# A gated linear attention kernel with two matmuls behind it: k turned by VectorE and put in order by way of DRAM, masks moved to ScalarE and GpSimd, a rounding moved behind the first scores

## The chip, the cores and the metric

The kernel runs on one core of a Trainium2 chip. The metric is the time of one execution in microseconds (us), the median of some runs. In profiles, PE is TensorE's matmuls, PEld its weight loads, DVE VectorE, ACT ScalarE, POOL GpSimd, SPq and ACTq the DMA issues in the streams of SyncE and ScalarE. L483 is a line of the kernel. The change shifts lines: the scores are L757 before and L770 after, the values L800 and L821, the states L815 and L837.

## The reference, cut to what matters

```python
def _attn_ref(q, k, v, alpha):          # (4, 8, 768, 48): batch, heads, tokens, head size
    state = np.zeros((B, H, D, D)); y = np.zeros_like(q)
    for t in range(S):
        state = alpha[:, :, t, :, None] * state + np.einsum('bhd,bhe->bhde', k[:, :, t], v[:, :, t])
        y[:, :, t] = np.einsum('bhd,bhde->bhe', q[:, :, t], state)
    return y
# x = y with the heads side by side: (3072, 384)
def _moe_ref(x, w_in, w_out):           # (384, 2048), (2048, 384)
    h = x @ w_in
    return ((h / (1 + np.exp(-h))) @ w_out)
```

## The kernel before

The tokens are cut into 24 chunks of 128 (6 per sequence, 4 sequences). For each chunk VectorE builds kp (k divided by its decay) and qp (q times its decay). Then TensorE does **scores** (kp times qp, masked to the causal half), **values** (masked scores times v, plus the running state times qp) and **states** (kp times v, added to the running state). The states need kp with tokens on partitions, so it has to be turned. Between these short pieces, one piece of the two big matmuls after another is put in, called `enter` (x times w_in) and `leave` (times w_out) here. From chunk 8 on (`NA`) the chunks run in a steady pattern.

```python
def scores(n):
    ps = c.pop("blank") if n >= NA else [ps_attn() for _ in range(2)]   # ps_attn: a ring of 3 PSUM buffers
    ...                                                                  # cut: 16 matmuls into ps
    for u in range(2):
        ...                                                              # cut: first chunks
        dve.tensor_tensor(g[:, u], ps[u], mask, ALU.mult)                # views cut
    if ci < NCH - 1:
        ps_k = ps_attn()
        for j in range(NP):
            pe.transpose(ps_k[:, j, :], c["kp"][:, j, :], ident)         # k turned by TensorE
        c["kn"] = work.tile([128, NP, C], F32, name="kn")
        act.copy(c["kn"], ps_k)

def load_v(n):                       # the v of chunk n, one of two buffers, three DMAs
    t = c["v"] = vns[n % NV]         # NV = 2: waits until the states of chunk n - 2 have read it
    nc.sync.dma_start(t[:, 0 : H // 2, 0:D], x[:, 0 : H // 2])
    ...

for step in range(STEPS):            # from chunk 8 on, in the order of the program:
    stages = [[(scores, 1)], [(products, 0)], [(values, 1), (states, 1)], [(quotient, 0), (blank, 0)]]
    for slot, group in enumerate(stages):
        for stage, lag in group:
            n = step - lag
            stage(n)
            if stage is quotient and n + 1 < NT: load(n + 1)      # alpha, k, q: 12 DMAs
            if stage is states and n + NV < NT: load_v(n + NV)
        fill(step, slot)             # pieces of the big matmuls
```

Two things here matter later. All these loads, and the stores of the output, are issued by **SyncE**, one after another. And the order of the program is not the order of an engine's instructions: when the kernel is built, each engine gets its own fixed order (the built order), which can change when the program does. How the builder chooses it was not looked into. On the chip, each engine goes through that order and waits where it must.

Of the kernel before, what the change touches and what calls it, by code (L numbers as in the profile page):

```python
# [8 lines left out]
F32 = mybir.dt.float32  # L9
# [346 lines left out]
def quotients(  # L356
# [22 lines left out]
    C = 128  # L379
# [27 lines left out]
    opool = pool("opool", 2)  # L407
    rpool = pool("rpool")
    upool = pool("upool")

# [118 lines left out]

    mask = consts.tile([128, 2, C], F32, name="mask")  # L530
    gps.memset(mask, 1.0)
    for odd in range(2):
        for e in range(2):
            m = mask[CH * e : CH * e + CH, odd, :]
            gps.affine_select(m, m, pattern=[[1, C]], compare_op=ALU.is_ge, fill=0.0,
                              base=-CH * (e ^ odd), channel_multiplier=-1)

# [56 lines left out]
    def weights(which):  # L594
# [18 lines left out]
        for i, (dst, src) in enumerate(pieces):  # L613
            if not wide:
                act.dma_start(dst, src)
                yield
                continue
            assert which == 0 or conv_done[0] == n_conv[0]
            bits = coming.pop(0)
            up = ahead.pop() if ahead else rounding(bits)  # L620
            hi, w = bits[:, :, 1], dst.bitcast(I32)
            tc.keep_in_program_order(
                dve.tensor_scalar(w, hi, 3, 0x3FFFFFFF, ALU.logical_shift_left, ALU.bitwise_and))
            dve.scalar_tensor_tensor(w, hi, -(1 << 30), w, ALU.bitwise_and, ALU.bitwise_or)
            dve.tensor_tensor(w, w, up, ALU.add)  # L625
            if i + 1 < len(pieces):
                ahead.append(rounding(coming[0]))
            fetch()
            yield
# [104 lines left out]

    def blank(n):

        if n < NA:
            return
        ps = ctxs[n]["blank"] = [ps_attn() for _ in range(2)]
        for t in ps:  # L740
            act.activation(t.rearrange("p j c -> p (j c)"), ident[:, 0:1].to_broadcast([128, 4 * C]),
                           AF.Copy, scale=0.0)

    def scores(n):
        c = ctxs[n]
        ci, b = c["ci"], c["b"]
        ps = c.pop("blank") if n >= NA else [ps_attn() for _ in range(2)]



        for j in (0, 2, 1, 3):
            for e in range(2 if n >= NA else 1):
                for u in range(2):
# [4 lines left out]
                              start=True, stop=True)  # L758
        g = c["g"] = work.tile([128, 2, NP, C], F32, name="g")
        for u in range(2):  # L760
            if n < GB:

                act.copy(g[:, u], ps[u])
                gps.affine_select(g[:, u], g[:, u], pattern=[[0, NP], [1, C]], compare_op=ALU.is_ge,  # L764
                                  fill=0.0, base=0, channel_multiplier=-1)
                continue
            m = mask[:, :, None, :] if n >= NA else mask[:, 0:1, None, :]
            dve.tensor_tensor(g[:, u].rearrange("p (o j) c -> p o j c", o=2),  # L768
                              ps[u].rearrange("p (o j) c -> p o j c", o=2),
                              m.to_broadcast([128, 2, NP // 2, C]), ALU.mult)  # L770
        if ci < NCH - 1:
            ps_k = ps_attn()
# [12 lines left out]
    def values(n):  # L785

        c = ctxs[n]
        ci, b, g, qp = c["ci"], c["b"], c["g"], c["qp"]
        vn = c["v"].rearrange("p (j u) d -> p j (u d)", u=2)
        s = st[b].rearrange("p j u e -> p j (u e)")  # L790
        py = ps_attn()
        todo = [(3 * j + i, vn[:, j, at : at + 32], g[:, u, j, :])
                for j in range(NP) for i, at, u in ((0, 0, 0), (1, 32, 0), (2, 80, 1))]
        todo += [(3 * j + 1, vn[:, j, 48:80], g[:, 1, j, :]) for j in range(NP)]
        if ci > 0:
# [10 lines left out]
    def states(n):  # L806
        c = ctxs.pop(n)
        ci, b, vn = c["ci"], c["b"], c["v"]
        if ci < NCH - 1:

            ps = ps_attn()
            for j in range(NP):
                for i in range(4):
                    r = slice(32 * i, 32 * i + 32)
                    pe.matmul(ps[r, j, 0:D], lhsT=c["kn"][:, j, r], rhs=vn[:, 2 * j + i // 2, 0:D],  # L815
                              start=True, stop=True)
# [288 lines left out]
    def settle():  # L1105

        first.close()
        late.update(look=pool("look"), part=pool("part"), xc=pool("xc"), turn=pool("turn"),
                    wx=pool("wx").tile([128, 8, NQ, 128], F32, name="wx"))
        quads = pool("quads")  # L1110
# [5 lines left out]
    def fill(step, slot):  # L1116

        at = step * SLOTS + slot
        if at < marks[0]:
            if step >= 1:  # L1120
                convert(0, (at - SLOTS) * 3 // (marks[0] - SLOTS) + 1)
            return
# [10 lines left out]
    for step in range(STEPS):  # L1133
# [6 lines left out]
        elif step >= NA:  # L1140
            stages = [[(scores, 1)], [(products, 0)], [(values, 1), (states, 1)], [(quotient, 0), (blank, 0)]]
        for slot, group in enumerate(stages):
            for stage, lag in group:
# [10 lines left out]
                if stage is states and n + NV < NT:  # L1154
                    load_v(n + NV)
            fill(step, slot)
            if step * SLOTS + slot >= NA * SLOTS - 1 and conv_done[1] == NFT and not late:
# [21 lines left out]
    ps = ps_attn()[0:1, 0, 0:1]  # L1179
    pe.matmul(ps, lhsT=good, rhs=mask[:, 0, C - 1 : C], start=True, stop=True)  # L1180
    dve.tensor_single_scalar(small, ps, 127.5, ALU.is_ge)
# [62 lines left out]
```

## Time and profile before

| what | before |
|---|---|
| time, median of 3 runs | 564.57 us |
| span of the profiled run | 561.6 us |
| TensorE busy | 543.9 us, so 17.7 us without a matmul |
| TensorE busy, 125 to 185 / 185 to 365 / 365 to 445 us | 60.00 / 179.26 / 80.00 us |
| VectorE, ScalarE, GpSimd busy | 453.0, 205.3, 15.1 us |

The prediction below shows the page's main lines. Two views that it didn't show also belong here. The first is the timeline of TensorE in the kernel before; the columns are start, length, engine, line, output and inputs, and count.

```profile
243.29 0.90 PE L757 MATMUL ps_a<-p,kp 48*64 48x128 f32 x32
244.12 0.66 PE L774 MATMUL ps_a<-ident,kp 128*128 128x128 f32 x4
...
255.09 1.08 PE L800 MATMUL ps_a<-g,vn 128*32 128x128 f32 x32
255.99 0.84 PE L800 MATMUL ps_a<-p,st 128*32 128x128 f32 x24
256.65 0.52 PE L815 MATMUL ps_a<-vn,kn 128*32 128x48 f32 x32
```

Scores and k's transposes come first, then 10.5 us of big matmuls (244.6 to 255.1), then the values, and the states directly behind them. The masking has those 10.5 us. The second is what SyncE's queue waits for (line waited for: us in total, times, longest):

```profile
SPq L996 <- DVE o L994: 72.2, 32, 5.9
...
SPq L482 <- PE ps_a L815: 31.0, 13, 5.1
```

L482 is the load of v; in 13 steps it stands at the head of SyncE's queue until the states (L815) have released its buffer, 5.1 us at most. L996 stores the output, which waits for VectorE.

### The profile page before, as it was taken

Reading aid. Unit: us, or ns where it says so; the run is one execution under the profiler, and the core shown is the slowest. Engines: PE = TensorE matmul, PEld = TensorE weight load, DVE = VectorE, ACT = ScalarE, POOL = GpSimd, SP = SyncE. Lnnn points to the kernel's source line nnn. Section 1 sums busy time; section 2 is a strip of 40 time slices with the busy share of each in tenths; the row PEclk is TensorE's granted clock in tenths of the full one; section 3 lists DMA queues with packets and bytes.
Section 4 is the critical chain, followed back from the end, with each engine's and each line's share of the span. In section 5 each row is a group of like instructions: output and inputs, shape, how many; then the busy total and the mean of one; then the engine's idle time right before and its main releaser. Section 6 shows DMA issues by size and latency. Waiting matters only on the chain.

```text
span 561.6 us, 12420 instructions
## 1 busy us (share of the span) xinstructions
PE 543.9 (97%) x5074; PEld 492.6 (88%) x5074; DVE 453.0 (81%) x829; ACT 205.3 (37%) x406; POOL 15.1 (3%) x36
## 2 busy tenths in 40 slices
PE   5899999999999999999999999999999999999996
PEld 3688887998999999899989999999998999899995
DVE  5797899966999799986998897899895875857731
ACT  2566543213233342443433443434443342332100
POOL 4211000100000000000000000000000000000000
PEclk9899999999999999999999999999999999999998
DMA  9989971143443333333425544435522123334200
GB/s 206 230 241 223 234 183 34 43 126 100 100 107 89 73 97 87 101 87 85 131 70 160 142 108 134 130 81 153 136 69 81 53 85 118 99 94 125 71 30 26
DMA packets 94417, 63.81 MB, mean 114 GB/s; under 512 B 55312, under 2 KB 86032, under 8 KB 94352
## 3 DMA queue, kind: packets, MB, share of 16 engines
q1 hardware_dynamic: 94352, 62.94, 43.3%
q8 instruction: 41, 0.67, 0.5%
q14 instruction: 24, 0.20, 0.1%
HBM read 58.20 MB, written 4.72 MB: 112 GB/s over the span
## 4 chain that ended last, share of the span: by engine, by line
PE 75%; DVE 14%; DMA 5%; SPq 2%; issue 2%; ACT 1%; POOL 0%; DVEq 0%; ACTq 0%
PE ps_o L980 33%; PE ps_m L882 18%; PE ps_m L858 11%; PE ps_a L800 6%; DMA bits<-in_moe_w_out_dram 3%; PE ps_a L757 3%; DVE seen L663 2%; PE ps_a L774 1%; DVE g L896 1%; DMA bits<-in_moe_w_in_dram 1%; DVE u L699 1%; PE ps_a L815 1%; DVE w_out L625 1%; DVE p L728 1%; SPq L456 1%
## 5 line engine op out<-in xcount | busy, mean ns | idle before, releaser
L980 PE MATMUL ps_o<-w_out,g 128*128 128x192 f32 x768 | 133.6, 328 | 1.1 <-DVE o L994 1.1
L980 PEld LDWEIGHTS ps_o<-w_out,g 128*128 128x128 f32 x768 | 125.5, 190 | 3.9 <-DVE o L994 1.5
L980 PE MATMUL ps_o<-wt,g 128*128 128x192 f32 x576 | 100.0, 327 | 0.0
L980 PEld LDWEIGHTS ps_o<-wt,g 128*128 128x128 f32 x576 | 95.1, 190 | 1.5
L858 PE MATMUL ps_m<-xt,w_in 128*128 128x256 f32 x384 | 88.5, 382 | 1.0 <-ACT xt L805 1.0
L858 PEld LDWEIGHTS ps_m<-xt,w_in 128*128 128x128 f32 x384 | 71.0, 190 | 11.0 <-ACT xt L805 1.4
L882 PE MATMUL ps_m<-xc,w_in 128*128 128x256 f32 x288 | 70.1, 379 | 0.0
L882 PEld LDWEIGHTS ps_m<-xc,w_in 128*128 128x128 f32 x288 | 54.0, 190 | 6.4 <-DVE g L896 0.2
L663 DVE TENSOR_REDUCE seen<-bits 128x1 f32<-128x384 int32 (+2 forms) x65 | 42.4, 689 | 16.8 <-DMA bits<-in_moe_w_out_dram 16.5
L893 ACT ACTIVATE g<-g 128x1024 f32<-128x1024 f32 x32 | 33.1, 1055 | 57.5 <-DVE g L896 57.5
L985 DVE TENSOR_TENSOR g<-g 128x512 f32<-128x512 f32 x72 | 48.5, 686 | 5.6 <-PE ps_o L980 5.6
L882 PE MATMUL ps_m<-xc,wx 128*128 128x256 f32 x192 | 50.1, 383 | 0.0
L888 ACT COPY g<-ps_m 128x512 f32<-128x512 f32 x64 | 36.8, 587 | 36.1 <-PE ps_m L882 36.0
L780 ACT ACTIVATE st<-st,least 128x96 f32<-128x96 f32 x80 | 24.1, 364 | 58.4 <-DVE least L702 58.4
L882 PEld LDWEIGHTS ps_m<-xc,wx 128*128 128x128 f32 x192 | 35.0, 190 | 4.2 <-issue 0.4
L896 DVE TENSOR_TENSOR g<-ps_m,g 128x512 f32<-128x512 f32 x56 | 37.4, 683 | 0.8 <-PE ps_m L882 0.5
L699 DVE TENSOR_TENSOR_SCAN u<-al,one 128x516 f32<-128x516 f32 x24 | 29.1, 1212 | 10.4 <-ACT al L696 10.3
L728 DVE TENSOR_TENSOR_SCAN p<-al,inv 128x516 f32<-128x516 f32 x24 | 29.4, 1226 | 5.2 <-PE ps_a L800 4.9
L861 ACT ACTIVATE g<-ps_m 128x512 f32<-128x512 f32 x32 | 19.0, 595 | 39.2 <-PE ps_m L858 39.0
L800 PE MATMUL ps_a<-g,vn 128*32 128x128 f32 x768 | 28.0, 282 | 3.9 <-POOL g L764 3.9
L800 PEld LDWEIGHTS ps_a<-g,vn 128*32 128x32 f32 x768 | 20.3, 112 | 11.2 <-issue 5.5
L768 DVE TENSOR_TENSOR g<-ps_a,mask 128x512 f32<-128x512 f32 x40 | 25.7, 685 | 4.0 <-PE ps_a L757 3.7
(125 smaller groups left out, 620.7 us busy)
## 6 DMA issues: line engine op xcount, KB each, us to landing
bits<-in_moe_w_in_dram SPq DMA_DIRECT2D x24, 512.0 KB, 4.7
bits<-in_moe_w_out_dram SPq DMA_DIRECT2D x32, 384.0 KB, 3.4
at<-in_alpha_dram SPq DMA_DIRECT2D x64, 96.0 KB, 2.4
kt<-in_k_dram SPq DMA_DIRECT2D x64, 96.0 KB, 2.6
qt<-in_q_dram SPq DMA_DIRECT2D x64, 96.0 KB, 2.5
bits<-in_alpha_dram SPq DMA_DIRECT2D x9, 512.0 KB, 3.8
out_dram<-o SPq DMA_DIRECT2D x48, 96.0 KB, 1.9
an<-in_alpha_dram SPq DMA_DIRECT2D x8, 192.0 KB, 5.1
```

Of the source, the lines that this page charges most:

```text
L663: dve.tensor_reduce(seen[kind][which][:, i : i + 1], x, axis=AX, op=op, apply_absolute_value=True))
L699: dve.tensor_tensor_scan(u[:, end - 1 :: -1], sg[:, end:0:-1], one[:, end:0:-1], 0.0, ALU.mult, ALU.add)
L728: dve.tensor_tensor_scan(p[:, 0:end], sg[:, 0:end], iv[:, 0:end], 0.0, ALU.mult, ALU.add)
L768: dve.tensor_tensor(g[:, u].rearrange("p (o j) c -> p o j c", o=2), ps[u].rearrange("p (o j) c -> p o j c", o=2), m.to_broadcast([128, 2, ...
L800: pe.matmul(py[32 * at : 32 * at + 32, t, :], lhsT=w, rhs=x, start=(i < 4), stop=(i >= len(todo) - 4), skip_group_check=True)
L858: pe.matmul(ps[:, e, :], lhsT=w_in[:, t, (f + e) * 128 : (f + e + 1) * 128], rhs=xt[:, t, :], start=(t == 0), stop=(t == NKT - 1))
L882: pe.matmul(ps[:, e], lhsT=block_w(w)[:, 2 * pair + e], rhs=block_x(grp, x), start=(first and e == 0), stop=(e == 1), skip_group_check=True)
L888: act.copy(to, ps)
L893: act.activation(x, x, AF.Silu)
L896: dve.tensor_tensor(to, a, b, op)
L980: pe.matmul(ps, lhsT=x, rhs=w[:, i], start=(first and i == 0), stop=(i == HF - 1), skip_group_check=True)
L985: dve.tensor_tensor(cells(grp, h, pair, *to), cells(grp, h, pair, *x), cells(grp, h, pair, *y), ALU.subtract)
```

## The change

Its intent is to take work off TensorE and VectorE. (1) From chunk 8 on, k is turned by VectorE in 32x32 blocks (`flip`) instead of by TensorE; a store to DRAM and four loads (`land`) put the blocks in order. (2) The causal mask is made by ScalarE's copies and GpSimd's selects instead of VectorE's multiplications. (3) At the start, one rounding of weights is traced behind the first scores.

```diff
+    dram = pool("dram", 2, bass.MemoryType.DRAM)
@@ the weights' conversion
             up = ahead.pop() if ahead else rounding(bits)
+            if which == i == 0:
+                yield
@@
-    def blank(n):                              # cut: its body
+    def flip(n):
+        c = ctxs[n]
+        if n < NA or c["ci"] == NCH - 1:
+            return
+        t = late["flip"].tile([128, 4, NP, 32], F32, name="flip")
+        dve.transpose(t, c["kp"].rearrange("p j (c i) -> p c j i", i=32))
+        c["flip"] = dram.tile([128, NP * C], F32, name="flips")
+        nc.sync.dma_start(c["flip"], t.rearrange("p c j d -> p (c j d)"))
+    def land(n):
+        c = ctxs[n]
+        if "flip" in c:
+            c["kn"] = work.tile([128, NP, C], F32, name="kn")
+            x = c.pop("flip").rearrange("(r d) (i x) -> i d r x", r=4, i=4)
+            for i in range(4):
+                nc.sync.dma_start(c["kn"][32 * i : 32 * i + 32], x[i])
@@ scores
-            m = mask[:, :, None, :] if n >= NA else mask[:, 0:1, None, :]
-            dve.tensor_tensor(...)             # cut: g = ps * m
-        if ci < NCH - 1:
+            x = ps[u].rearrange("p (o j) c -> p o j c", o=2)
+            act.copy(swapped[:, :, u, :, CH:], x[:, :, :, CH:])
+            for r, o in earlier:
+                act.copy(swapped[r, o, u, :, 0:CH], x[r, o, :, 0:CH])
+        if n >= NA:
+            for at, half in ((0, earlier), (CH, later)):
+                for r, o in half:
+                    x = swapped[r, o].rearrange("p u j c -> p (u j) c")[:, :, at : at + CH]
+                    gps.affine_select(x, x, ...)
+        if n < NA and ci < NCH - 1:
             ps_k = ps_attn()                   # TensorE's transposes, now for the first chunks only
@@
-            stages = [[(scores, 1)], [(products, 0)], [(values, 1), (states, 1)], [(quotient, 0), (blank, 0)]]
+            stages = [[(land, 1), (scores, 1)], [(products, 0)], [(values, 1), (states, 1)],
+                      [(quotient, 0), (flip, 0)]]
```

More of the change, by code (lines that the diff above doesn't have):

```diff
@@ L526, in quotients @@
         gps.memset(t, 0.0)
-    mask = consts.tile([128, 2, C], F32, name="mask")
-    gps.memset(mask, 1.0)
-    for odd in range(2):
-        for e in range(2):
-            m = mask[CH * e : CH * e + CH, odd, :]
-            gps.affine_select(m, m, pattern=[[1, C]], compare_op=ALU.is_ge, fill=0.0,
-                              base=-CH * (e ^ odd), channel_multiplier=-1)
+    decayed = fix.tile([128, 2 * NP * C], F32, name="g")
+    low, high = slice(0, CH), slice(CH, C)
+    earlier, later = [(low, 0), (high, 1)], [(low, 1), (high, 0)]
+    ones = consts.tile([128, 1], F32, name="ones")
+    gps.memset(ones, 1.0)
     st = [fix.tile([128, NP, 2, D], F32, name=f"st{b}") for b in range(B)]
@@ L733, in quotient @@
         dve.tensor_tensor(qp, q, qp, ALU.mult)
-    def blank(n):
-        if n < NA:
+    def flip(n):
+        c = ctxs[n]
+        if n < NA or c["ci"] == NCH - 1:
             return
-        ps = ctxs[n]["blank"] = [ps_attn() for _ in range(2)]
-        for t in ps:
-            act.activation(t.rearrange("p j c -> p (j c)"), ident[:, 0:1].to_broadcast([128, 4 * C]),
-                           AF.Copy, scale=0.0)
+        t = late["flip"].tile([128, 4, NP, 32], F32, name="flip")
[9 more added lines that the diff above has]
+                nc.sync.dma_start(c["kn"][32 * i : 32 * i + 32], x[i])
     def scores(n):
@@ L746, in scores @@
         ci, b = c["ci"], c["b"]
-        ps = c.pop("blank") if n >= NA else [ps_attn() for _ in range(2)]
+        ps = [ps_attn() for _ in range(2)]
         for j in (0, 2, 1, 3):
@@ L758, in scores @@
                               start=True, stop=True)
-        g = c["g"] = work.tile([128, 2, NP, C], F32, name="g")
+        g = decayed.rearrange("p (u j c) -> p u j c", u=2, j=NP)
+        swapped = decayed.rearrange("p (o u j c) -> p o u j c", o=2, u=2, j=NP // 2)
+        c["g"] = (lambda u, j: g[:, u, j, :]) if n < NA else (
+            lambda u, j: swapped[:, j // 2, u, j % 2, :])
         for u in range(2):
-            if n < GB:
+            if n < NA:
                 act.copy(g[:, u], ps[u])
@@ L766, in scores @@
                 continue
-            m = mask[:, :, None, :] if n >= NA else mask[:, 0:1, None, :]
-            dve.tensor_tensor(g[:, u].rearrange("p (o j) c -> p o j c", o=2),
-                              ps[u].rearrange("p (o j) c -> p o j c", o=2),
-                              m.to_broadcast([128, 2, NP // 2, C]), ALU.mult)
-        if ci < NCH - 1:
+            x = ps[u].rearrange("p (o j) c -> p o j c", o=2)
[6 more added lines that the diff above has]
+                    x = swapped[r, o].rearrange("p u j c -> p (u j) c")[:, :, at : at + CH]
+                    gps.affine_select(x, x, pattern=[[0, NP], [1, CH]],
+                                      compare_op=ALU.is_ge, fill=0.0, base=0, channel_multiplier=-1)
+        if n < NA and ci < NCH - 1:
             ps_k = ps_attn()
@@ L787, in values @@
         c = ctxs[n]
-        ci, b, g, qp = c["ci"], c["b"], c["g"], c["qp"]
+        ci, b, g, qp = c["ci"], c["b"], c.pop("g"), c["qp"]
         vn = c["v"].rearrange("p (j u) d -> p j (u d)", u=2)
@@ L791, in values @@
         py = ps_attn()
-        todo = [(3 * j + i, vn[:, j, at : at + 32], g[:, u, j, :])
+        todo = [(3 * j + i, vn[:, j, at : at + 32], g(u, j))
                 for j in range(NP) for i, at, u in ((0, 0, 0), (1, 32, 0), (2, 80, 1))]
-        todo += [(3 * j + 1, vn[:, j, 48:80], g[:, 1, j, :]) for j in range(NP)]
+        todo += [(3 * j + 1, vn[:, j, 48:80], g(1, j)) for j in range(NP)]
         if ci > 0:
@@ L814, in states @@
                     r = slice(32 * i, 32 * i + 32)
-                    pe.matmul(ps[r, j, 0:D], lhsT=c["kn"][:, j, r], rhs=vn[:, 2 * j + i // 2, 0:D],
+                    kn = c["kn"][:, j, r] if n < NA else c["kn"][:, i, 32 * j : 32 * j + 32]
+                    pe.matmul(ps[r, j, 0:D], lhsT=kn, rhs=vn[:, 2 * j + i // 2, 0:D],
                               start=True, stop=True)
@@ L1108, in settle @@
         late.update(look=pool("look"), part=pool("part"), xc=pool("xc"), turn=pool("turn"),
+                    flip=pool("flip"),
                     wx=pool("wx").tile([128, 8, NQ, 128], F32, name="wx"))
@@ L1119, in fill @@
         if at < marks[0]:
-            if step >= 1:
+            if at == SLOTS:
+                next(conv[0])
+            elif step >= 1:
                 convert(0, (at - SLOTS) * 3 // (marks[0] - SLOTS) + 1)
@@ L1155, in quotients @@
                     load_v(n + NV)
+            if step * SLOTS + slot == NA * SLOTS + 3:
+                x = decayed.rearrange("p (o i c) -> p o i c", o=2, c=C)
+                for r, o in later:
+                    gps.memset(x[r, o, :, 0:CH], 0.0)
             fill(step, slot)
@@ L1179, in quotients @@
     ps = ps_attn()[0:1, 0, 0:1]
-    pe.matmul(ps, lhsT=good, rhs=mask[:, 0, C - 1 : C], start=True, stop=True)
+    pe.matmul(ps, lhsT=good, rhs=ones, start=True, stop=True)
     dve.tensor_single_scalar(small, ps, 127.5, ALU.is_ge)
```

## The prediction

> **What bounds the kernel now.** I read the page's busy line first, then the slices, then the chain.
>
> ```profile
> PE 543.9 (97%) x5074; PEld 492.6 (88%) x5074; DVE 453.0 (81%) x829; ACT 205.3 (37%) x406; POOL 15.1 (3%) x36
> PE   5899999999999999999999999999999999999996
> PE 75%; DVE 14%; DMA 5%; SPq 2%; issue 2%; ACT 1%; POOL 0%; DVEq 0%; ACTq 0%
> ```
>
> TensorE is busy in every slice but the first two and the last, its weight loads too, and the chain of waits is three quarters TensorE. So the kernel is TensorE's stream in program order; what doesn't shorten that stream, or one of its few gaps, changes nothing. The busy times by stretch show where gaps are: from 0 to 23 us TensorE is busy 14.2 us, from 185 to 365 us it is busy 179.26 of 180, from 365 to 445 us all 80.
>
> The second question is how near VectorE is to binding. The same view, with stretches of one step (one attention chunk, 21.6 us) each:
>
> ```profile
> 190.00:211.60 21.60, 21.60 (x228) 20.07 (x220) 21.04 (x43) 9.97 (x22) 0.00 (x0) 1.00 0.33 83
> 211.60:233.30 21.70, 21.30 (x217) 18.88 (x217) 21.24 (x44) 5.87 (x12) 0.00 (x0) 1.00 0.37 93
> 233.30:255.00 21.70, 21.70 (x225) 20.26 (x224) 17.17 (x29) 12.05 (x24) 0.00 (x0) 1.00 0.32 83
> 255.00:276.80 21.80, 21.80 (x245) 19.87 (x248) 19.13 (x33) 6.62 (x13) 0.00 (x0) 1.00 0.44 117
> ```
>
> The columns after the length are TensorE, its weight loads, VectorE, ScalarE, GpSimd. VectorE has steps at 97% (21.04 of 21.60) and steps at 79%. The steps at 97% are where TensorE has its two only gaps of the middle (0.40 and 0.34 us, at 232.2 and 294.9 us). So VectorE is close behind, and the change must not load it.
>
> **What the Trainium skill says.** "Perfetto Trace Analysis", section Identifying the Most-Contended Engine: the busy share of matmuls is a bad measure of TensorE's distance from its limit, the share of weight loads is a better one. Here that is 88%, which agrees with the reading above. "VectorE: DVE Perf Modes", section The three transpose paths: VectorE turns only 32x32 blocks, TensorE a full 128x128 into PSUM. The change has to order the blocks in another way (by DRAM) for that reason; the trace has VectorE's turn of 128x512 at 1.11 us (48 of them). "DMA: Bandwidth & Descriptors", section Anatomy of one DMA: about 2 us fixed per transfer, mostly the receipt of the write. Here 96 KB stores land in a median 1.9 us and 96 KB loads in 2.4 to 2.6. "SBUF — State Buffer", section Who interferes with whom: a VectorE instruction with two SBUF inputs and a GpSimd instruction that reads SBUF exclude each other for a whole instruction. The trace agrees:
>
> ```profile
> 32.86 1.93 POOL L764 TENSOR_SCALAR_AFFINE_SELECT g<-g 128x512 f32<-128x512 f32 x2 [10.46 <-ACT g L763]
> 33.29 1.00 DVE L624 SCALAR_TENSOR_TENSOR w_in<-bits,w_in 128x512 int32<-128x512 int32 x1
> 34.43 0.90 DVE L625 CUSTOM_DVE_ANT_0 w_in<-w_in,up 128x1024 uint16<-128x1024 uint16 x1
> ```
>
> Two selects took 1.93 us here, against 1.23 us for a pair at 21.17 us with VectorE idle; the two VectorE instructions took 1.00 and 0.90 us against their usual 0.69. So a select costs VectorE about 0.25 us (0.31 + 0.21 over two).
>
> **The change, part 1: k turned by VectorE.** It applies to the chunks from 8 on that have a successor (8 to 19): 12 chunks. TensorE loses 4 transposes in each. Their busy time (0.66 us) is not what they cost. I compare two stretches of the same make, one with and one without transposes:
>
> ```profile
> 265.08 0.90 PE L757 MATMUL ps_a<-p,kp 48*64 48x128 f32 x32
> 265.91 0.66 PE L774 MATMUL ps_a<-ident,kp 128*128 128x128 f32 x4
> 266.40 2.77 PE L980 MATMUL ps_o<-w_out,g 128*128 128x192 f32 x16
> 269.00 1.03 PE L882 MATMUL ps_m<-xc,wx 128*128 128x256 f32 x4
> ...
> 434.67 0.90 PE L757 MATMUL ps_a<-p,kp 48*64 48x128 f32 x32
> 435.50 2.87 PE L980 MATMUL ps_o<-w_out,g 128*128 128x192 f32 x16
> 438.21 1.03 PE L882 MATMUL ps_m<-xc,wx 128*128 128x256 f32 x4
> ```
>
> From the scores' start to the start of the group after next: 269.00 - 265.08 = 3.92 us with, 438.21 - 434.67 = 3.54 us without. The step out of the scores into full matmuls costs 0.10 us (2.87 against 2.77) and now falls on the next group. So 0.38 us a chunk, 12 x 0.38 = **4.6 us off TensorE's stream**. ScalarE loses 12 copies of 0.585 us, all beside TensorE. VectorE gains 12 turns of 1.11 us = 13.3 us. The way through DRAM: turn done about at 240.5 us in the step of 233 us, a 256 KB store of some 2.5 us, four 64 KB loads of some 2.5 us plus their issue (0.4 us each): about 247.5 us. The states that read it start at 256.7. Some 9 us of slack, so hidden; 6.3 MB more on DMA engines that are 40% busy there.
>
> **Part 2: masks.** In chunks 8 to 23 VectorE loses 2 multiplications of 0.685 us (32 in all, 21.9 us), ScalarE loses 2 blankings of 0.60 us (19.2 us) and gains 6 small copies. From 0.315 us at 192 and 0.475 at 384 elements I estimate 0.37 and 0.26 us for 256 and 128 elements: 2 x (0.37 + 2 x 0.26) = 1.8 us a chunk. GpSimd gains 4 selects of 64x512, at the 0.61 to 0.97 us of a 128x512 one. Chunks 4 to 7 go from VectorE's 2 multiplications to 2 copies and 2 selects. After the scores (end 244.1 us) the copies end about 246.5 and the selects by 250; the values start at 255.1. Hidden, with about 4 us in hand. Nothing of this was on TensorE's path, so the direct gain is 0; I give 0.2 us for the relief at 65 to 125 us, where TensorE idles 1.2 us for VectorE and ScalarE.
>
> VectorE's sum in chunks 8 to 19: -1.37 + 1.11 + 4 x 0.25 x (the share of its work with two SBUF inputs, some 0.7) = +0.4 us a step. In the steps at 97% this spills into the next. I take **1.0 us of new TensorE gaps** over twelve steps.
>
> **Part 3: rounding behind first scores.**
>
> ```profile
> 11.39 0.69 ACT L609 ACTIVATE up<-bits 128x512 int32<-128x512 uint32 x1 [1.92 <-DMA bits<-in_moe_w_in_dram]
> 13.73 0.67 ACT L609 ACTIVATE up<-bits 128x512 int32<-128x512 uint32 x1 [1.65 <-DMA bits<-in_moe_w_in_dram]
> 14.30 1.05 ACT L763 COPY g<-ps_a 128x512 f32<-128x512 f32 x2
> 14.94 1.94 POOL L764 TENSOR_SCALAR_AFFINE_SELECT g<-g 128x512 f32<-128x512 f32 x2 [7.91 <-ACT g L763]
> 15.89 0.64 PE L800 MATMUL ps_a<-g,vn 128*32 128x128 f32 x4 [3.62 <-POOL g L764]
> ```
>
> The first scores are done by 11.7 us, but their copies stand in ScalarE's order behind the second rounding, which waits for a DMA until 13.73. Now only the first rounding (to 12.1 us) is ahead: copies at 12.1, selects at 12.7, values at 13.6 instead of 15.9, **up to 2.3 us**. It won't all last. From 23.2 to 48.7 us VectorE converts w_in back to back, just in time for TensorE, and one rounding at 38.06 had waited 1.07 us for its bytes, with the DMA engines 85 to 113% busy. I count 1.6 us.
>
> **Sum:** 4.6 + 1.6 + 0.2 - 1.0 = 5.4 us; 564.6 - 5.4 = **559.2 us**, 1.0% faster.
>
> **The rivals.** (a) VectorE becomes the bound: selects lock it out more than 0.25 us each (say 0.6), +1.5 us a step in steps that have 0.3 to 0.6 us free. For it: the 97% steps. Against it: the neighbours at 79 to 88% take the spill, and many instructions read PSUM or have one input. It would eat 3 to 5 us: 562 to 564. (b) The values wait for the selects, or the states for k from DRAM, because one in-order queue (ScalarE behind a wait, SyncE behind a store) holds them. For it: ScalarE waited up to 6.7 us for VectorE in this trace, SyncE up to 6.1. Against it: 4 and 9 us of slack. One us in each of 16 chunks would bring it to about 570 at worst. (c) The start is bound by DMA after all, the 2.3 us vanish by 48 us: 560.8. (d) VectorE's relief removes all gaps and the start keeps 2.3 us: 557.
>
> **Range and chances.** 556.5 to 563.5 holds (a), (c), (d) and the run-to-run spread of 1.5 us. Faster by 2% needs 553.3, beyond what the removed work and all gaps named can give: 0.04. Slower by 2% needs a failure like (b) twice over: 0.02. Within 2%: 0.94.
>
> **What would show it.** Part 1: no transposes of kp after chunk 7, the stretch of scores plus next group at 3.54 us in chunks 8 to 19, no TensorE wait at the states. Part 2: no TensorE wait for GpSimd after 60 us; selects ending 4 us or more ahead of the values; VectorE's busy time about 13 us lower. Part 3: the first values at about 13.6 us, and the eighth w_in group of TensorE (now at 51.86) some 1.6 us earlier. Wrong would be: gaps of TensorE in the middle that sum to over 3 us, or a reordered TensorE stream with more switches between small and full matmuls.

## The result, and the profile after

The changed kernel took **592.35 us** (median of 4 runs, 589.6 to 596.22) against 564.22 us before on the same chip, and is correct. The ratio is 1.0503 with a 95% interval of 1.0442 to 1.0565: **5% slower**. A ratio here is the mean time of one kernel's fast runs over that of the other's in the same rounds, so not quite the ratio of the quoted medians. All runs compared in this document are fast ones.

The page of the changed kernel, its busy line, slices and chain:

```profile
PE 551.2 (93%) x5026; PEld 491.2 (83%) x5026; DVE 446.2 (76%) x801; ACT 211.8 (36%) x466; POOL 53.4 (9%) x106
...
PE   6999999999989889799899899879899989999996
...
PEclk9999999999999999899999999979999999999999
...
PE 52%; DVE 22%; DMA 13%; issue 4%; ACT 4%; POOL 2%; SPq 1%; DVEq 0%; ACTq 0%; POOLq 0%
```

TensorE now has holes all through the middle (the 8s and 7s), and in the two slices with a 7 the granted clock dips too. The chain that ended last is half TensorE, where it was three quarters; VectorE and DMA have taken the rest. TensorE's idle time is 590.6 - 551.2 = 39.4 us against 17.7, so 21.7 us more. Its busy time is 7.3 us longer although 48 transposes are gone. The two make up the span's difference, 590.6 - 561.6 = 29.0 us. By stretch (the columns are length, TensorE, weight loads, VectorE, ScalarE, GpSimd, granted clock, DMA share, GB/s), in the changed kernel:

```profile
125.00:185.00 60.00, 56.63 (x635) 50.55 (x624) 44.75 (x82) 16.80 (x47) 7.22 (x14) 1.00 0.40 106
185.00:365.00 180.00, 168.15 (x1704) 150.11 (x1703) 144.83 (x251) 68.66 (x161) 18.11 (x32) 0.99 0.43 114
365.00:445.00 80.00, 69.97 (x625) 60.64 (x624) 62.49 (x107) 31.10 (x67) 5.42 (x12) 0.96 0.44 111
```

All of this lies from chunk 8 on: 3.4, 11.9 and 10.0 us without a matmul, against 0, 0.7 and 0. No engine has become the bound: VectorE is less busy too, 144.83 us of 180 against 160.03, and ScalarE, 68.66 against 73.50; GpSimd, with the new selects, is busy 18.11 us. When none is full and the time is longer, the engines are waiting for each other, so I read what is waited for. First SyncE's queue, which the prediction had looked at for its longest wait alone:

```profile
SPq L483 <- PE ps_a L837: 88.7, 13, 11.4
SPq L1018 <- DVE o L1016: 69.9, 21, 9.6
```

The load of v (L483) now holds the head of SyncE's queue for 88.7 us in all, 13 times as before, but up to 11.4 us each. Second, TensorE's waits: the largest is

```profile
PE ps_a L821 <- POOL g L790: 15.8, 10, 3.0
```

the values waiting for GpSimd's selects, in 10 of the 16 chunks. One step of the timeline of the changed kernel, all engines, has both:

```profile
226.77 0.91 SPq L466 DMA_DIRECT2D at<-in_alpha_dram  x2
...
230.39 0.67 DVE L745 STREAM_TRANSPOSE flip<-kp 128x512 f32<-128x512 f32 x1
...
235.95 0.55 PE L837 MATMUL ps_a<-vn,kn 128*32 128x48 f32 x32
...
236.39 0.39 SPq L483 DMA_DIRECT2D vn<-in_v_dram  x1
...
236.43 0.90 PE L770 MATMUL ps_a<-p,kp 48*64 48x128 f32 x32
236.72 2.00 ACT L915 ACTIVATE g<-g 128x1024 f32<-128x1024 f32 x2 [0.33 <-DVE g L918]
...
238.24 1.98 SPq L466 DMA_DIRECT2D kt<-in_k_dram  x4
...
238.63 0.35 ACT L783 COPY g<-ps_a 128x256 f32<-128x256 f32 x1
...
239.95 2.64 POOL L790 TENSOR_SCALAR_AFFINE_SELECT g<-g 64x256 f32<-64x256 f32 x4 [19.98 <-ACT g L783]
...
240.31 1.80 SPq L466 DMA_DIRECT2D qt<-in_q_dram  x4
...
242.21 0.38 SPq L747 DMA_DIRECT2D flips<-flip  x1
...
242.64 1.94 PE L821 MATMUL ps_a<-g,vn 128*32 128x128 f32 x32 [2.96 <-POOL g L790]
...
244.99 2.01 SPq L755 DMA_DIRECT2D kn<-flips  x3
```

Read it along SyncE. At 227.7 its queue comes to the load of v and stands, 8.7 us, until the states at 235.95 have read the old v. Only at 236.39 does it go on: v, then k and q of the next chunk, then, at 242.21, the store of the turned k. VectorE had that tile ready at 231.1, so it lay in the queue for 11 us. Its last landing load is issued about 247 us. The next states start late again, at 259.70, but TensorE doesn't wait for the turned k there: in all twelve steps the last landing load had been issued 7.7 to 14.5 us ahead of the states, and none took over 3.7 us to land. The states' late place is in TensorE's built order. Then read it along TensorE: the states have come away from the values and stand directly ahead of the next chunk's scores. The values (242.64) follow the scores after five big matmuls only, too soon for ScalarE's copies, which had stood behind a 2 us activation, and for the 2.64 us of selects. TensorE stands 2.96 us and then runs the values at nearly half speed, 1.94 us against 1.08 for the same matmuls at 265.43.

That order is not the chip's doing. This is TensorE's built order for one step (chunk 14's scores first; number of matmuls in the program, of which the trace records two each, transposes excepted):

```
before:   scores 16; turn k 4; enter 6; leave 8; enter 6; leave 8; values 28; states 16; enter 6; leave 8; enter 6
changed:  scores 16; leave 13; values 28; enter 3; leave 8; enter 6; leave 8; enter 6; leave 6; states 16
```

In the step before this one the changed kernel has only 5 matmuls between scores and values, where the old one has 26. The 10 steps in which TensorE waits for the selects are the 10 of the 16 with 9 big matmuls or fewer in that place; the 6 with 11 or more have no such wait.

The wait in SyncE's queue reaches TensorE as well, by way of VectorE. The chain of work in a later step, in order of time, as the profile puts it:

```profile
377.63 0.48 PE ps_a L837 x32
...
379.01 0.41 SPq L485
...
381.72 4.26 DMA kt<-in_k_dram
...
386.64 0.98 DVE al L676
...
388.03 1.12 PE ps_m L904 x4
```

The late states (L837) let v's load go, the loads behind it land late, VectorE's turn of the next alpha (L676) is late for them, and behind it in VectorE's order stands a sum of a group (xc) that TensorE's big matmuls wait for, 3.36 us here.

### The profile page after: what moved, and what is told of

Read it like the earlier page. It is cut to its first block, busy times and chain, and to the rows that moved or that the text cites. A ratio compares the mean times of both kernels' runs of the same rounds, so it can differ in the third digit from the quotient of the medians.

```text
span 590.6 us, 12596 instructions
## 1 busy us (share of the span) xinstructions
PE 551.2 (93%) x5026; PEld 491.2 (83%) x5026; DVE 446.2 (76%) x801; ACT 211.8 (36%) x466; POOL 53.4 (9%) x106
## 4 chain that ended last, share of the span: by engine, by line
PE 52%; DVE 22%; DMA 13%; issue 4%; ACT 4%; POOL 2%; SPq 1%; DVEq 0%; ACTq 0%; POOLq 0%
PE ps_o L1002 22%; PE ps_m L880 11%; PE ps_m L904 9%; DMA bits<-in_moe_w_out_dram 6%; PE ps_a L821 4%; DVE seen L665 4%; DVE g L918 3%; DVE turn L676 2%; PE ps_a L770 2%; POOL g L790 2%; DMA at<-in_alpha_dram 1%; DMA kt<-in_k_dram 1%; DVE u L701 1%; DVE al L676 1%; PE ps_a L837 1%
## 5 line engine op out<-in xcount | busy, mean ns | idle before, releaser
L1002 PE MATMUL ps_o<-w_out,g 128*128 128x192 f32 x768 | 136.0, 329 | 1.3 <-DVE o L1016 1.1
L1002 PE MATMUL ps_o<-wt,g 128*128 128x192 f32 x576 | 101.3, 327 | 0.0
L880 PEld LDWEIGHTS ps_m<-xt,w_in 128*128 128x128 f32 x384 | 71.0, 190 | 11.4 <-ACT xt L826 1.6
L904 PE MATMUL ps_m<-xc,w_in 128*128 128x256 f32 x288 | 74.0, 390 | 3.2 <-DVE xc L562 1.4
L665 DVE TENSOR_REDUCE seen<-bits 128x1 f32<-128x384 int32 (+2 forms) x65 | 42.5, 689 | 28.6 <-DMA bits<-in_moe_w_out_dram 17.2
L790 POOL TENSOR_SCALAR_AFFINE_SELECT g<-g 64x256 f32<-64x256 f32 x64 | 33.7, 548 | 315.4 <-ACT g L783 314.4
L915 ACT ACTIVATE g<-g 128x1024 f32<-128x1024 f32 x32 | 33.3, 1055 | 56.4 <-DVE g L918 56.4
L821 PE MATMUL ps_a<-g,vn 128*32 128x128 f32 x768 | 29.0, 288 | 16.3 <-POOL g L790 15.8
```

Of the source, the lines that this page charges most:

```text
L665: dve.tensor_reduce(seen[kind][which][:, i : i + 1], x, axis=AX, op=op, apply_absolute_value=True))
L790: gps.affine_select(x, x, pattern=[[0, NP], [1, CH]], compare_op=ALU.is_ge, fill=0.0, base=0, channel_multiplier=-1)
L821: pe.matmul(py[32 * at : 32 * at + 32, t, :], lhsT=w, rhs=x, start=(i < 4), stop=(i >= len(todo) - 4), skip_group_check=True)
L880: pe.matmul(ps[:, e, :], lhsT=w_in[:, t, (f + e) * 128 : (f + e + 1) * 128], rhs=xt[:, t, :], start=(t == 0), stop=(t == NKT - 1))
L904: pe.matmul(ps[:, e], lhsT=block_w(w)[:, 2 * pair + e], rhs=block_x(grp, x), start=(first and e == 0), stop=(e == 1), skip_group_check=True)
L915: act.activation(x, x, AF.Silu)
```

## The experiments

**The theory** (the loop): late states keep v's buffer, v's load stands at the head of SyncE's in-order queue, the store and the landing loads of the turned k stand behind it, so the next states are late. (The trace above already limits its last link: it can act only where the orders are built, for on the chip the states never waited for the turned k.) **The rivals**: VectorE is overloaded by the turn and the selects (its load); GpSimd's masks hold the values up on their own; late states by themselves cost the time, whatever the queue does. A later one: the place of the groups' sums (`sums_x`) in VectorE's order. Where a text on record for x9 to x12 uses letters, C is that last rival and D is VectorE's load.

All results, against the kernel before in the same rounds (its median was 562.99 to 564.22 us):

| run | what | us, median | ratio, 95% interval |
|---|---|---|---|
| x1_masks | part 2 alone | 563.15 | 0.9990 [0.9979, 1.0002] |
| x2_flip | part 1 alone | 593.19 | 1.0523 [1.0505, 1.0540] |
| x3_round | part 3 alone | 561.62 | 0.9966 [0.9954, 0.9977] |
| x4_notrip | changed, no way through DRAM (wrong result) | 560.81 | 0.9951 [0.9934, 0.9968] |
| x5_trip_act | changed, that way issued by ScalarE | 560.45 | 0.9941 [0.9924, 0.9958] |
| x6_trip_pool | the same, by GpSimd | 561.54 | 0.9956 [0.9942, 0.9971] |
| x7_v_pool | changed, v loaded by GpSimd | 562.99 | 0.9980 [0.9969, 0.9992] |
| x8_flip_act_round | parts 1 (by ScalarE) and 3 | 561.50 | 0.9964 [0.9950, 0.9978] |
| x9_act_sums | x5, group sums later | 561.12 | 0.9951 [0.9935, 0.9968] |
| x10_states_late | before, states late | 581.56 | 1.0326 [1.0297, 1.0354] |
| x11_round_sums | x3, group sums later | 562.84 | 0.9977 [0.9968, 0.9986] |
| x12_flip_act_sums | x8, group sums later | 565.04 | 1.0018 [1.0007, 1.0030] |
| x13_notrip_late | x4, states late (wrong result) | 559.07 | 0.9931 [0.9907, 0.9954] |
| x14_store_first | changed, store ahead of the loads | 577.95 | 1.0263 [1.0241, 1.0285] |
| x15_v_behind | changed, v behind the landing | 574.33 | 1.0180 [1.0153, 1.0208] |
| x16_both | x14 and x15 at once | 568.97 | 1.0102 [1.0077, 1.0127] |
| **x17_act_late** | x5, states late | **557.13** | 0.9890 [0.9865, 0.9916] |

### Which part: x1, x2, x3

Each is the kernel before with one part of the change.

```diff
# x1: only the mask's lines of the diff      # x3: "if which == i == 0: yield", and the step that runs what follows it (cut above)
# x2: only flip, land and the stages; VectorE keeps its masks and ScalarE its blanking
-            stages = [[(scores, 1)], [(products, 0)], [(values, 1), (states, 1)], [(quotient, 0), (blank, 0)]]
+            stages = [[(land, 1), (scores, 1)], [(products, 0)], [(values, 1), (states, 1)],
+                      [(quotient, 0), (flip, 0), (blank, 0)]]
```

> The kernel before with part 2 alone: ScalarE copies, GpSimd selects, no blanks; k still turned by TensorE, rounding as before. Theory A (the trip of k through DRAM puts the states late in TensorE's fixed order, the v loads that wait for the states block SyncE's queue ahead of the k and q loads, so the scores come late and the values follow them too closely): values follow the scores by 20 or more big matmuls as before, no TensorE wait for GpSimd in the middle, 561 to 566 us. Theory B (the chain of copies and four selects, 2.4 us in all at GpSimd, is too long for the kernel, whatever the order): TensorE waits for GpSimd at the values by 1 to 3 us a chunk, 580 to 595 us.

> The kernel before with part 1 alone: k turned by VectorE and ordered through DRAM on SyncE's queue; masks stay VectorE multiplications with blanks, rounding as before. Theory A: states directly ahead of the next scores in TensorE's order, values 5 to 12 big matmuls behind the scores, SyncE waits at the v loads of over 80 us in total (31 before), TensorE waits at the values for VectorE's masks; 575 to 595 us. Theory B: near 560 us (4.6 us of transposes less).

> The kernel before with part 3 alone: the first rounding split from its piece. Both theories: first values at about 13.6 us in place of 15.9, 562 to 564 us (1 to 2 us less than before); 564.5 if the start is bound by DMA.

Part 1 alone has the whole loss, 593.19 us; in its trace SyncE waits 89.2 us at v's load. The waits at the values for VectorE's masks, which were expected there, are only 1.9 us in all: TensorE has 15.6 us more without a matmul than before (33.3), spread over waits for VectorE, and its matmuls are busy 14.4 us longer (558.3 us; the granted clock was 0.91 from 365 to 445 us). So the loss doesn't need the selects. Part 2 alone costs nothing, so the selects don't hold up the values by themselves; the 15.8 us wait for them in the changed kernel goes with the order. Part 3 alone gives 2.1 us. In its timeline the first values start at 14.35 us, where they started at 15.89:

```profile
14.35 0.64 PE L802 MATMUL ps_a<-g,vn 128*32 128x128 f32 x4 [0.33 <-POOL g L766]
```

### What in part 1: x4, x5, x6, x7

```diff
# x4: the states read VectorE's blocks as they are (a wrong result on purpose)
-        c["flip"] = dram.tile([128, NP * C], F32, name="flips")
-        nc.sync.dma_start(c["flip"], t.rearrange("p c j d -> p (c j d)"))
+        c["kn"] = t.rearrange("p c j d -> p c (j d)")
# x5 (x6: nc.gpsimd in place of nc.scalar)
-        nc.sync.dma_start(c["flip"], t.rearrange("p c j d -> p (c j d)"))
+        nc.scalar.dma_start(c["flip"], t.rearrange("p c j d -> p (c j d)"))
-                nc.sync.dma_start(c["kn"][32 * i : 32 * i + 32], x[i])
+                nc.scalar.dma_start(c["kn"][32 * i : 32 * i + 32], x[i])
# x7: the three DMAs of load_v from chunk 8 on by nc.gpsimd, the way through DRAM stays with nc.sync
```

> The changed kernel without the trip through DRAM: the states read VectorE's turned blocks as they are. The result is wrong on purpose (blocks in the wrong order in chunks 8 to 19). All else of the change stays, copies, selects and turns too. Theory A: the states stand behind the values again, 557 to 561 us. Theory B: no better than 580 us, as the selects are all there.

> The changed kernel with one thing moved: the store and the four loads of the trip are issued from ScalarE's queue, not SyncE's. Theory A1 (a loop through SyncE's in-order queue: late states hold the v load, that holds the k and q loads and the store of the next turned k, that makes the next states late): the loop is cut, states directly behind the values, SyncE waits at the v loads near 31 us as before, 557 to 563 us. Theory A2 (the latency of the trip itself makes the states late, on any queue): states still late, 575 us or more.

> As x5, but from GpSimd's queue. A1: 557 to 565 us; GpSimd's wait for the store to land can hold the selects behind it, so up to 3 us over x5. A2: 575 us or more.

> The changed kernel with the trip left on SyncE's queue, but the v loads of chunks 8 on issued from GpSimd's. A1: cut at the other link, the k and q loads no longer wait for the states; states may stand later than in the kernel before, yet the values keep 12 or more big matmuls from the scores; 557 to 566 us. A2: 575 us or more, as the trip is the same.

With VectorE's turn but no trip (x4, relative error 0.151, as meant), the loss is gone. With the whole trip, the same 6.3 MB and 60 DMAs, but issued from another engine (x5, x6), it is gone too, and the result is right. So neither VectorE's load nor the transfers cost 30 us; sharing SyncE's queue does. Taking v's load out of that queue instead (x7) does nearly as well. With either the trip or v's load elsewhere, one no longer waits behind the other. SyncE's wait at v's load falls to 28.6 us in x5, and TensorE's built order is regular again, values and states together. In x7 the built order has the states 18 to 29 big matmuls behind the values in the first five steps, then 9, 2 and from there 0; in the changed kernel it is 27 to 44 in all twelve. That fits a loop that acts where the orders are built.

But queue and built order changed together in every one of these runs. No run keeps the changed kernel's TensorE order and frees the queue, so how much of the 30 us is the order and how much the waits on the chip is not shown.

### The rest against x3: x8, x9, x11, x12

x5 is only 1.2 us faster than part 3 alone, where part 1 was to give 4.6. In x5's trace TensorE is busy 176.99 us of 180 from 185 to 365 us, against 179.26 before, and its waits include 3.3 us for VectorE's qp. x8 leaves part 2 out, to see whether GpSimd's selects slow VectorE. The other three trace the groups' sums later, out of the way of qp, with x11 as a control without part 1.

```diff
# x8: before + parts 1 and 3, flip and land by nc.scalar
# x9, x11, x12: in x5, x3, x8
+            if pieces[done][1] == 0 and slot == 2 and step < NT:
+                break                            # the piece of sums waits for the next slot
```

> A candidate that should beat both: the kernel before with parts 1 and 3, the trip on ScalarE's queue, masks left with VectorE. A1: 2.1 us of part 3 and up to 4.6 us of transposes less than before: 557 to 561 us. A2: 575 us or more.

> x5 with one thing more: the sums of a new group (11 VectorE additions) are traced behind q's product with its decay, not ahead of it. Theory C (x5 loses most of the 4.6 us of the removed transposes because in the steps with sums q's product comes late, behind them, and the scores wait for it: TensorE idle 3.0 us from 185 to 365 us, 0.75 before): these waits go, TensorE idle there under 1.5 us, 557.5 to 559.5 us. Theory D (the gaps are VectorE's load, whatever the order): 560 to 561.5 us, as x5.

> A control for x9: x3 with the sums behind q's product. In the kernel before q's product stood ahead of the sums anyway and TensorE had 0.74 us of gaps in the middle: 561 to 562 us, as x3, under C and D.

> x8 with the sums behind q's product: parts 1 and 3, the trip on ScalarE's queue, masks by VectorE multiplications. C: 558 to 560 us; VectorE carries the masks too, so 0.5 to 1 us over x9. D: 561 to 562 us, as x8.

x8 comes to 561.50, just above the 557 to 561 expected; its interval overlaps that of x5, so part 2 helps or hurts little here. Moving the sums was a miss: x9 is no better than x5 (TensorE busy 177.31 of 180), x11 no better than x3, and x12 at 565.04 far from the 558 to 560 of C and over the 561 to 562 of D too. The wait of the scores for qp fell from 3.3 us in x5 to 0.5 in x9, but other waits came in its place, 1.2 us of them for a sum. So the place of the sums is not the cause. What goes with it is VectorE being nearly full in those steps; I didn't measure that by itself.

### Late states by themselves: x10, x13

x10 is the kernel before with the states put directly ahead of the next scores.

```diff
# x10
-            stages = [[(scores, 1)], [(products, 0)], [(values, 1), (states, 1)], [(quotient, 0), (blank, 0)]]
+            stages = [[(states, 2), (scores, 1)], [(products, 0)], [(values, 1)], [(quotient, 0), (blank, 0)]]
+            if step == NA: stages[0] = stages[0][1:]
# x13: the same in x4, (flip, 0) in place of (blank, 0)
```

> The kernel before with one thing changed on purpose: the states of a chunk stand directly ahead of the next chunk's scores in TensorE's order, as the changed kernel has them; no trip, no turns, masks as before. Late states alone do harm: 575 us or more. Theory A1 (they harm only by way of the v loads that hold other transfers of the loop on SyncE's queue; without the store and loads of a trip behind them there is no loop): 563 to 568 us, values 20 or more big matmuls behind the scores.

It missed: 581.56 us, as if late states alone cost 18 us. But its trace has a wait that the changed kernel hasn't, k's transposes on TensorE for a PSUM buffer that the states still hold:

```profile
PE ps_a L774 <- DVE st L821: 15.2, 12, 1.8
```

There are three such buffers: the states hold one until VectorE has added it, the scores take two, and the transposes need another. The changed kernel has no such transposes from chunk 8 on, so this test was not clean. x13 is the clean one: late states, no transposes, no trip.

> The changed kernel without the way through DRAM (the states read the turned blocks from VectorE's tile; wrong result on purpose), with the states traced behind the next step, so that TensorE's built order has them directly ahead of the next scores, as in the changed kernel, while no store or landing load stands in SyncE's queue. There are no transposes of k, so no fourth score buffer is wanted. The loop theory (late states harm only because the trip's store and loads stand in the same queue as the v, k and q loads) expects 560 to 566 us. The rival, late states alone (their late release of the v buffer holds up the k and q loads in SyncE's queue), expects 575 us or more and over 60 us of SyncE waiting for states.

559.07 us, and TensorE without a gap to speak of:

```profile
185.00:365.00 180.00, 179.59 (x1832) 162.94 (x1831) 162.79 (x287) 74.10 (x170) 14.37 (x32) 1.00 0.41 109
```

Late states are harmless by themselves; its SyncE waits 17.7 us at v's load. This rival falls, for an order that keeps the values 14 to 28 big matmuls behind the scores from the second step on, as x13's does.

### What in the queue: x14, x15, x16

These keep everything on SyncE and change only where things stand in its queue.

```diff
# x14 (and x16): the next alpha, k, q behind the store of the turned k
-                if stage is quotient and n + 1 < NT:
+                if stage is (flip if step >= NA else quotient) and n + 1 < NT:
                     load(n + 1)
# x15 (and x16): v behind the landing loads, one slot later
-                if stage is states and n + NV < NT:
+                if step < NA and stage is states and n + NV < NT:
                     load_v(n + NV)
+            if step > NA and slot == 0 and step - 2 + NV < NT:
+                load_v(step - 2 + NV)
```

> The changed kernel with the next chunk's alpha, k and q loads traced behind the store of the turned k, all still on SyncE's queue: in the built queue the store now stands ahead of these loads and of the v load. If the store's 12 us in the queue is the link that closes the loop, the time falls to 575 us or less. If it is the k and q loads behind the v load's wait that cost, it stays at 585 us or more.

> The changed kernel with each v load traced behind the landing loads of the turned k, one slot later, all still on SyncE's queue: in the built queue the v load stands behind the k and q loads and the store, not ahead of them. If the v load's wait for the states at the head of the queue is what feeds the loop, the time falls to 575 us or less and SyncE's wait for states below 50 us. If it is the queue's mere length (13 issues of 0.4 us and more a step), it stays at 585 us or more.

> The changed kernel with both reorderings at once on SyncE's queue: the store ahead of the next alpha, k and q loads, and the v load behind the landing loads. If the two losses of x14 and x15 are two links of one loop, and those orders are all of it, the time falls to 566 us or less. If other waits at the head of the queue (an output store of the previous group that waits for VectorE, up to 10 us in x15) and its length are part of it, it stays between 568 and 574 us.

The store's place gives back 14.4 us of the 28 (x14, a little short of what was expected), v's place 18.0 us (x15), both 23.4 us (x16); these are differences of medians from different chips. So with the order in the queue most of the loss goes, and neither link alone is all of it. (In x15's and x14's built queues v stands between the store and the landing loads, or among the alpha loads, not quite where the program has it.) x16 still misses its 566 us and lies in the range of the text's rival, 568 to 574: it is 6 us slower than before, 8.5 us slower than x5. SyncE's wait for states at v's load is down to 10.9 us in x15 and hardly there in x16, and yet the built order has the states 22 to 43 big matmuls behind the values in x15; so v's wait isn't all that keeps them late. In x15 the place at the head is taken by other waits, such as two stores of the output, in its timeline of SyncE:

```profile
233.17 10.56 SPq L1018 DMA_DIRECT2D out_dram<-o  x2
```

Those two stores spanned 10.56 us of the queue, most of it a wait for VectorE's data (up to 9.7 us in one), and alpha, k, q and the turned k came behind. In x16 SyncE's waits have the store of the turned k itself, now ahead of the loads:

```profile
SPq L747 <- DVE flip L745: 31.9, 7, 11.9
```

Whatever stands ahead waits for somebody. I take that for the rest of x16's loss, but no run isolates it; TensorE's waits for the selects are still 6.4 us there.

### A better version: x17

x13 was the fastest, but wrong. x17 is x5 with the same late states.

```diff
-            stages = [[(land, 1), (scores, 1)], [(products, 0)], [(values, 1), (states, 1)],
+            stages = [[(states, 2), (land, 1), (scores, 1)], [(products, 0)], [(values, 1)],
                       [(quotient, 0), (flip, 0)]]
+            if step == NA: stages[0] = stages[0][1:]
```

> x5 (the trip on ScalarE's queue, a correct result) with the states traced one step later, so that TensorE's built order is that of x13, states directly ahead of the next scores. If late states are harmless and give the trip more slack, it comes to 557 to 560.5 us and beats x5. If the trip on ScalarE costs TensorE gaps that lie elsewhere (VectorE's load), it stays at 560 to 562 us. Over 570 us would say that late states do hurt.

**557.13 us**, correct, 1.1% faster than the kernel before by the ratio, and 5.9% faster than the changed one by the two medians (from different chips). Its page and its stretch:

```profile
PE 542.5 (98%) x5026; PEld 489.6 (88%) x5026; DVE 443.5 (80%) x801; ACT 210.7 (38%) x466; POOL 48.5 (9%) x106
```

```profile
185.00:365.00 180.00, 179.06 (x1826) 162.42 (x1826) 162.86 (x286) 74.69 (x171) 15.24 (x32) 1.00 0.48 134
```

Against the changed kernel TensorE is idle 13.3 us, not 39.4, and the same 5026 matmuls are busy 8.7 us less. The order is the one that looked like the culprit, states directly ahead of the scores: 16 scores, 28 big matmuls, 28 values, 20 big matmuls, 16 states (26 and 22 in the steps between). Why it beats x5 isn't tested. One thing goes with it: the wait for qp (3.3 us in x5, and in x4) isn't among its waits, nor among x13's.

## Why the prediction was wrong, point by point

It said 559.2 us (556.5 to 563.5), with 0.02 for slower by over 2%; it was 592.35.

**The step that failed** is in part 1: "about 247.5 us. The states that read it start at 256.7. Some 9 us of slack, so hidden". It timed the trip as if SyncE's queue were free, and took the places of states and values in TensorE's stream as given ("TensorE's stream in program order"). In the changed kernel the turn was even done earlier, 28.6 us ahead of the states that use it (231.1 and 259.70), where I had 16.2. But its store waited 11 us in the queue, and the issue of the last landing load came 16 us after the turn, where I had its arrival 7 us after. That delay by itself was still hidden: no TensorE wait at the states shows in the trace, as predicted, because the built order has them 27 to 44 big matmuls behind the values, later than the data comes. What was not hidden is what came with it. v's load waited for these late states and held SyncE's queue for 88.7 us. And the values stood 5 to 16 big matmuls behind the scores, 5 to 7 in nine steps, where before it was 12 to 28, so part 2's "the values start at 255.1. Hidden, with about 4 us in hand" failed too: TensorE waited 15.8 us for the selects.

**Rival (b)** named the right object, "one in-order queue (… SyncE behind a store) holds them", and capped it wrongly at 570 us. It counted slack per chunk, in the old order. It missed that late states release v late, that v's load stands in the same queue, and that the next loads and the next turned k stand behind it. It also priced delay at the values and states alone, while k and q, and with them VectorE and the scores, came late too. x5 to x7 show that the loss needs both in one queue, x14 to x16 that it depends on their order there; that the delay is handed on from step to step is not shown on the chip. The sentence on what would be wrong, "gaps of TensorE in the middle that sum to over 3 us, or a reordered TensorE stream", describes what came, but got 0.02.

**Part 1's gain** was right in the stretch that it was read from. The trace of x17 has the stretch from scores to the group after next:

```profile
262.65 0.90 PE L770 MATMUL ps_a<-p,kp 48*64 48x128 f32 x32
263.48 2.87 PE L1002 MATMUL ps_o<-w_out,g 128*128 128x192 f32 x16
266.19 1.03 PE L904 MATMUL ps_m<-xc,wx 128*128 128x256 f32 x4
```

266.19 - 262.65 = 3.54 us, as predicted. The turn was mis-sized: 0.70 us, not 1.11, because I took the duration of a turn with another layout. By the ratios x17 is about 4.3 us faster than x3, which has part 3 alone (an estimate, from different chips), close to the 4.6 us.

**Part 2** is right in its direct gain of 0 (x1: within the noise). In the changed kernel it is wrong that TensorE never waits for GpSimd after 60 us (15.8 us). VectorE's busy time fell by 6.8 us, not 13 (9.5 in x17). The selects are of 64x256, not 64x512 as the prediction has it, and take 0.66 us each (2.64 us for four), within its 0.61 to 0.97; the copies were sized right (0.35 and 0.27 us).

**Part 3** is right: first values at 14.39 us (13.6 predicted), the eighth group of w_in at 50.10 us instead of 51.86, so 1.76 us earlier (1.6 predicted), 2.1 us in the time of x3.

**The new gaps**, "1.0 us", are mis-sized even without the loop: x5 has 0.56 + 3.01 + 0.86 = 4.4 us of idle TensorE from 125 to 445 us against 0.74 before, so about 3.7 us of new ones. In x17 it is 0.27 + 0.94 + 0 = 1.2 us, 0.5 us of new ones. There the whole gain, 562.99 - 557.13 = 5.9 us, is close to the 5.4 us of the prediction's sum.

**Still open**: how the 30 us divide between the built order and the waits in the queue on the chip, why matmuls take longer beside the gaps, what x16's last 6 us are made of, why x5 has gaps for VectorE that x17 hasn't, and how the builder came to the changed order.

## What to carry to other kernels

Before adding a transfer to an engine's queue, list what stands in that queue and what each entry waits for; a DMA that is short and early by itself is as late as the longest wait ahead of it. Look for a ring: if what the transfer brings releases, later on, something that the same queue waits for, a slack read from the old kernel's order says little, for that order may not last. Issue such a transfer from another engine's queue, and compare the built order of the bounding engine before and after, for a stream's order is not yours to assume.

## What the Trainium skill lacked or had wrong

- "DMA: Bandwidth & Descriptors", section Issuing engines are not separate DMA queues, says that initiating DMAs on several engines only saves the sequencer's time to initiate them, "which is usually small relative to the DMA itself". Here the same DMAs issued by ScalarE in place of SyncE moved the time from 592.35 to 560.45 us. The section doesn't say what a DMA that waits for its semaphores does to those behind it in the same engine's stream: v's load held SyncE for 88.7 us in all; of one store's 11 us in the queue, 5.3 us were that wait and 5.8 us the loads that had stood in front of it.
- "VectorE: DVE Perf Modes", section The three transpose paths, gives one duration, for bf16. It lacks one for f32. Of 128x512 the runs show two, for two layouts: 1.10 us for the loads' strided turn, 0.70 us (0.67 to 0.77, 12 of them) for the turn of kp.
- No page that I read says what the order of a loop's transfers in one engine's queue can cost; the runs show 14.4 us for one reordering (x14), 18.0 us for the other (x15) and 23.4 us for both (x16).
